# Attention and two gated layers on one core: the tokens' split and turn moved from TensorE to DMA, and two steps on V placed behind a slice

## The chip, the cores and the metric

One core of one Trainium2 chip runs the whole program. The metric is the device time of one execution in microseconds. TensorE (PE) multiplies, VectorE (DVE) and ScalarE (ACT) work on elements, GpSimd (POOL) reduces over partitions, and SyncE (SP) issues every DMA of this kernel on one queue. PEld is TensorE's weight load, which overlaps with its matmuls.

## The reference, cut to what matters

Attention over 4 batches of 8 heads with 576 tokens of width 64, mixed with a retrieval from a memory; then, over all 2304 tokens of width 512, an RMS norm with a gated layer (SiLU), and a second gated layer (sigmoid). The hidden width of both is 1536.

```python
a = softmax(scale * q @ k.T, causal)
attn = g * (phi(q) @ M_prev) / (phi(q) @ z_prev) + (1 - g) * (a @ v)     # per head
x = attn.transpose(0, 2, 1, 3).reshape(2304, 512)
xn = x / sqrt(mean(x * x) + 1e-6) * rms_g
h = silu(xn @ w_gate) * (xn @ w_val)
x = h @ w_out
out = (sigmoid(x @ w_gate2) * (x @ w_val2)) @ w_out2
```

## The kernel before

**Groups.** Tokens are worked in five groups. Group -1 holds the first 128 tokens of all four batches (512 tokens). Groups 0 to 3 hold the other 448 tokens of one batch each. A group runs the two gated layers one after the other (`l` = 0 and 1), and each layer goes over `NF` = 12 slices of 128 hidden units: a gate product (`pg`) and a value product (`pv`), both in `mm3` at L786 with 12 matmuls each, the elementwise part in `hidden` (tanh at L803, products at L805 to L813, a high half on ScalarE at L818 or L822 and a low half on VectorE at L819 or L823), and the slice's share of the output (`po`, `out_share`, L839), which is computed after the products of the next slice. Every operand is split into a high and a low half, so that one product takes three matmuls. Weights pass through a ring of 13 slots (`slot`), three a slice, loaded by SyncE (L753, L756). At the end of a layer `evacuate` empties the four output banks, and in the second layer stores them.

**Attention of the next batch.** While group `g` runs its 24 slices, the attention of group `g + 1` is computed beside it. `att_steps` (L905) yields 36 steps in order: the load of V (`att_v`, L137 and L138), then for the heads `att_qk` (loads and splits q and k) and `att_scores` (scores, maximum over partitions at L501, softmax weights into the single tile `pt`); after head 0's scores `att_vmax` (step 3 counted from 0: five maxima over V at L146, one maximum over partitions, a scale), after head 1's scores `att_vsplit` (step 6: V into a high half on ScalarE, L169, and a low half on VectorE, L170), one head later `att_av` (weighted sum, L517 to L519), and for each pair of heads `att_mem`. The last five steps are `att_norm` (L595 to L588) and four times `next_xT`, which calls `att_xT`. The loop at L1019 emits these steps after the output shares, in proportion to the slices done: in groups 0 to 2 step 3 comes up in slice 3 of the first layer, step 6 in slice 4.

**The tokens' turn.** `att_xT` (L602) takes one tile of 128 tokens: L605 multiplies by the norm and `rms_g` into `xn` (two buffers), four TensorE transposes (L610) turn it into a PSUM tile of the pool `psa` (two buffers, shared with scores and sums), ScalarE copies the fp16 high half out (L614), VectorE subtracts for the low half (L615). The fourth tile of a group gives 64 tokens only. The first gate product of the next group reads all tiles.

**What sets the order.** Each engine runs its instructions in one fixed order. The framework's scheduler lays it out at build time from its own estimate of when each instruction is ready, preferring what was emitted earlier. So an instruction may stand a good deal before or behind the place where it is emitted. `tc.issue_after(i)` keeps all instructions emitted inside it that run on `i`'s engine behind `i` in that engine's order; it adds no semaphore.

Of the kernel before, what the change touches and what calls it, by code (L numbers as in the profile page):

```python
# [9 lines left out]
F32 = mybir.dt.float32  # L10
F32R = mybir.dt.float32r
F16 = mybir.dt.float16
# [4 lines left out]
ALU = mybir.AluOpType  # L17
# [39 lines left out]
def attn_moe_moe_kernel(ctx, tc, qT, kT, qk0, v, mz, beta, w8, rms_g, outT):  # L57
# [6 lines left out]
    nc = tc.nc  # L64
    B, H, D, S = qT.shape
    NP = H // 2
    DM = H * D
    KD = DM // 128
    NF = w8.shape[1]
# [6 lines left out]
    ap_ = ctx.enter_context(tc.tile_pool(name="ap", bufs=1))  # L76
# [7 lines left out]
    ident = const.tile([128, 128], F32, name="ident")  # L84
# [4 lines left out]
        out=tri, in_=tri, compare_op=ALU.is_ge, fill=NEG, base=0, pattern=[[1, 128]], channel_multiplier=-1  # L89
# [35 lines left out]
    for i in range(2):  # L125
        t = const.tile([128, S], F32R, name=f"q2_{i}")
# [6 lines left out]
    st = {}  # L133
# [468 lines left out]
    def att_xT(g, t, xt):  # L602
        s = st[g]
        xn = ap_.tile([128, DM], F32, tag="xn", bufs=2, name="xn")
        nc.vector.scalar_tensor_tensor(  # L605
            out=xn, in0=s["x"][:, t, :], scalar=s["ri"][:, t:t + 1], in1=g_bc, op0=ALU.mult, op1=ALU.mult
        )
        ps = late["ps"].tile([128, KD, 128], F32, tag="pa", name="pxt")
        for k in range(KD):
            nc.tensor.transpose(ps[:, k, :], xn[:, k * 128:(k + 1) * 128], ident)  # L610
        o = 64 if t == 3 else 0
        c0 = 128 * t
        n = 128 - o
        nc.scalar.copy(out=xt[0][:, :, c0:c0 + n], in_=ps[:, :, o:128])  # L614
        nc.vector.tensor_tensor(  # L615
            out=xt[1][:, :, c0:c0 + n], in0=ps[:, :, o:128], in1=xt[0][:, :, c0:c0 + n], op=ALU.subtract
        )


    late, first_raw = {}, []  # L620
    ring = {"w": 0, "top": 0, "raw": 0}
# [45 lines left out]
    def is_half(g, l, f):  # L667
        return g >= 0 and (l == 0 or f >= NWIDE)
# [29 lines left out]
    for i in range(2):  # L698
        t = const.tile([128, 512], I32, name=f"top{i}")
# [82 lines left out]
    def mm3(ps, w, x, n, o=0):  # L782
        i = 0
        for k in range(KD):
            for a, b in ((0, 0), (0, 1), (1, 0)):
                nc.tensor.matmul(  # L786
                    ps[:, 0:n], w[:, a, k * 128:(k + 1) * 128], x[b][:, k, o:o + n], start=(i == 0), stop=(i == 3 * KD - 1)
                )
                i += 1

    def hidden(w, l, f, n, g, x, h, o=0):


        pg = late["mm"].tile([128, NMAX], F32, tag="mm", name="pg")
        mm3(pg, w[0], x, n, o)
        pv = late["mm"].tile([128, NMAX], F32, tag="mm", name="pv")
        mm3(pv, w[1], x, n, o)

        t, hh = h
        t = t[:, o:o + n]  # L800
        half = is_half(g, l, f)
        u = unit[0 if l == 0 else 2][:, f]
        nc.scalar.activation(out=t, in_=pg[:, 0:n], func=AF.Tanh, scale=u[:, 0:1] if half else 0.5)  # L803
        if l == 0:
            nc.vector.scalar_tensor_tensor(out=t, in0=t, scalar=1.0, in1=pg[:, 0:n], op0=ALU.add, op1=ALU.mult)  # L805
            if half:
                nc.vector.scalar_tensor_tensor(  # L807
                    out=t, in0=t, scalar=kappa[:, f:f + 1], in1=pv[:, 0:n], op0=ALU.mult, op1=ALU.mult
                )
            else:  # L810
                nc.vector.tensor_tensor(out=t, in0=t, in1=pv[:, 0:n], op=ALU.mult)
        else:
            nc.vector.scalar_tensor_tensor(out=t, in0=t, scalar=1.0, in1=pv[:, 0:n], op0=ALU.add, op1=ALU.mult)  # L813
        if hh is None:
            return
        hi, lo = hh[:, 0, 0:n], hh[:, 1, 0:n]
        if l == 0 or g < 0:
            nc.scalar.copy(out=hi, in_=t)  # L818
            nc.vector.tensor_tensor(out=lo, in0=t, in1=hi.bitcast(F32), op=ALU.subtract)  # L819
        else:  # L820
            c = u[:, 1:2] if half else 0.5
            nc.scalar.activation(out=hi, in_=t, func=AF.Copy, scale=c)  # L822
            nc.vector.scalar_tensor_tensor(  # L823
                out=lo, in0=t, scalar=c, in1=hi.bitcast(F32), op0=ALU.mult, op1=ALU.subtract
            )
# [70 lines left out]
    def wide_tokens(tags):  # L896

        return [xp.tile([128, KD, NMAX], F32R, tag=t, name="x" + t) for t in tags]

    def half_tokens(tag):  # L900

        t = xp.tile([128, 2, KD, NMAX], F16, tag=tag, name="h" + tag)
        return [t[:, 0], t[:, 1]]

    def att_steps(g):  # L905
        yield lambda: att_v(g)

        for h in range(H + 1):
            if h < H:
                yield lambda h=h: att_qk(g, h)  # L910
                yield lambda h=h: att_scores(g, h)

            if h == 0:
                yield lambda: att_vmax(g)
            if h == 1:
                yield lambda: att_vsplit(g)
            if h > 0:
                yield lambda h=h: att_av(g, h - 1)
                if h % 2 == 0:
                    yield lambda h=h: att_mem(g, h // 2 - 1)  # L920
        yield lambda: att_norm(g, 0, 4)
        for t in range(4):
            yield lambda t=t: next_xT(g, t)
# [33 lines left out]
    def next_xT(g, t):  # L957
        if t == 0:
            st["xt"] = half_tokens("a")
        att_xT(g, t, st["xt"])  # L960

    xt, early_ws, early_hs = att_first()
    zctx.close()
# [11 lines left out]
    for g in range(-1, B):  # L975
        n = 512 if g < 0 else S - 128
        steps = list(att_steps(g + 1)) if g + 1 < B else []

        total = 2 * NF - (6 if g < 0 else 4)

        wait = 1 if g < 0 else 0
        done, used = 0, 0
        for l in range(2):
            early = 2 if g < 0 and l == 0 else 0
            ws, hs = early_ws[:early], early_hs[:early]
            for f in range(early):
                hidden(ws[f], l, f, 256, g, xt, hs[f], 256)
            po = None
            for f in range(NF + 1):
                if f < NF:  # L990
                    if f >= early:
                        if g > 0 and l == 1 and f == NWIDE:
                            mid = NF if g < B - 1 else NF // 2 + 2
                            for e, c in ((nc.vector, slice(NWIDE, mid)), (nc.gpsimd, slice(mid, NF))):
                                if c.start < c.stop:
                                    e.tensor_scalar(
                                        out=unit[2][:, c],
                                        in0=unit[1][:, c],
                                        scalar1=st["half_is1"],
                                        scalar2=None,  # L1000
                                        op0=ALU.mult,
                                    )
                        ws.append(weights(g, l, f))
                        hs.append(htiles(g, l, f))
                        hidden(ws[f], l, f, n, g, xh if l == 1 and is_half(g, l, f) else xt, hs[f])
                if f > 0:
                    if po is None:
                        po = [late[f"po{d // 2}"].tile([128, NMAX], F32, tag=f"po{d}", name="po") for d in range(KD)]
                    out_share(ws[f - 1], hs[f - 1], po, f - 1, n)
                    done += 1  # L1010
                    with ExitStack() as after:

                        if g < 0 and done < 5:
                            traced = nc.cur_bb.bb.instructions
                            for e in (mybir.EngineType.Activation, mybir.EngineType.DVE, mybir.EngineType.SP):
                                after.enter_context(
                                    tc.issue_after(next(i for i in reversed(traced) if i.engine == e))
                                )
                        while used < len(steps) and used < len(steps) * (done - wait) // (total - wait):  # L1019
                            steps[used]()  # L1020
                            used += 1
            if g < 0 and l == 0:
                begin.close()
            xn = wide_tokens("cd") if l == 0 else None
            for d in range(KD):
                evacuate(l, d, n, g, po[d], xn)
            if l == 0 and g >= 0:
                xh = half_tokens("b")
                halve_tokens(n, po, xh)
            if l == 0 and g < 0:  # L1030
                token_scale()
            xt = xn
        xt = st.pop("xt", None)
# [55 lines left out]
```

## Time and profile before

| | us |
|---|---|
| median of 3 runs | 1075.39 |
| lowest to highest | 1075.17 to 1077.75 |
| the profiled execution | 1077.86 |
| its span, first to last instruction | 1076.1 |
| TensorE busy in the span | 1043.3 |
| VectorE busy | 738.0 |
| ScalarE busy | 551.1 |

All rows of the profile below are of that one execution, and their times count from the start of its span. A timeline line gives the start, the length, the engine, the source line, the operation with output and inputs, and the count of merged instructions; the bracket at its end is how long the engine stood before it and what ended that. Lengths of merged matmuls overlap with the next line, because matmuls are pipelined. Waits are put down to the releaser that came last.

### The profile page before, as it was taken

Reading aid. Unit: us, or ns where it says so; the run is one execution under the profiler, and the core shown is the slowest. Engines: PE = TensorE matmul, PEld = TensorE weight load, DVE = VectorE, ACT = ScalarE, POOL = GpSimd, SP = SyncE. Lnnn points to the kernel's source line nnn. Section 1 sums busy time; section 2 is a strip of 40 time slices with the busy share of each in tenths; the row PEclk is TensorE's granted clock in tenths of the full one; section 3 lists DMA queues with packets and bytes.
Section 4 is the critical chain, followed back from the end, with each engine's and each line's share of the span. In section 5 each row is a group of like instructions: output and inputs, shape, how many; then the busy total and the mean of one; then the engine's idle time right before and its main releaser. Section 6 shows DMA issues by size and latency. Waiting matters only on the chain.

```text
span 1076.1 us, 17841 instructions
## 1 busy us (share of the span) xinstructions
PE 1043.3 (97%) x6505; PEld 756.1 (70%) x6509; DVE 738.0 (69%) x1588; ACT 551.1 (51%) x1074; POOL 93.1 (9%) x85
## 2 busy tenths in 40 slices
PE   7899999999899999998999999999999999999998
PEld 5778887888666677665677876766777766667665
DVE  5969999998788788885747876485687653224211
ACT  4768877776587658763434553353346332112111
POOL 2301012000011011100101010000010100000000
PEclk8999999999999999999999999999999999999999
DMA  6499998985567855875547445555554445454440
GB/s 263 149 361 375 323 351 269 329 274 169 191 225 263 284 177 152 283 237 198 166 136 218 149 155 171 183 182 159 186 171 132 132 138 174 146 184 157 142 133 34
DMA packets 90679, 218.49 MB, mean 203 GB/s; under 512 B 10720, under 2 KB 16864, under 8 KB 90464
## 3 DMA queue, kind: packets, MB, share of 16 engines
q1 hardware_dynamic: 90592, 217.36, 61.5%
q8 instruction: 51, 0.84, 0.3%
q14 instruction: 36, 0.29, 0.1%
HBM read 173.28 MB, written 44.04 MB: 202 GB/s over the span
## 4 chain that ended last, share of the span: by engine, by line
PE 71%; DVE 12%; DMA 9%; ACT 4%; issue 3%; SPq 1%; POOL 0%; ACTq 0%; DVEq 0%; POOLq 0%
PE pg L786 21%; PE po L839 21%; PE pv L786 20%; PE ps L206 3%; DMA w<-kept 2%; DMA x<-in_v 1%; DMA rawl<-in_w 1%; DMA g_bc<-in_rms_g 1%; PE pm L566 1%; DMA qd<-in_qT 1%; PE pav L517 1%; PE pav L519 1%; PE pav L518 1%; DVE vl L170 1%; ACT sc L197 1%
## 5 line engine op out<-in xcount | busy, mean ns | idle before, releaser
L803 ACT ACTIVATE t<-pg,unit 128x448 f32<-128x448 f32 x88 | 55.5, 630 | 148.2 <-PE pg L786 148.0
L839 PE MATMUL po<-h,ws 128*128 128x448 f32 (+1 forms) x504 | 121.1, 384 | 0.0
L839 PEld LDWEIGHTS po<-h,ws 128*128 128x128 f32 x504 | 93.3, 188 | 11.9
L501 POOL PARTITION_ALL_REDUCE mb<-mx x32 | 60.2, 1881 | 466.0 <-DVE mx L497 448.7
L786 PEld LDWEIGHTS <-wr 128*128 128x128 f16 x648 | 60.2, 98 | 56.8 <-issue 6.1
L786 PEld LDWEIGHTS <-ws 128*128 128x128 f16 x624 | 58.2, 98 | 54.8 <-issue 5.5
L813 DVE SCALAR_TENSOR_TENSOR t<-t,pv 128x448 f32<-128x448 f32 (+1 forms) x60 | 37.9, 632 | 84.0 <-PE pv L786 83.3
L839 PE MATMUL po<-h,wl 128*128 128x448 f32 (+1 forms) x384 | 93.8, 386 | 0.2 <-DVE h L823 0.2
L839 PE MATMUL po<-h,wr 128*128 128x448 f32 x360 | 83.7, 377 | 0.7 <-DVE h L819 0.7
L786 PEld LDWEIGHTS <-wl 128*128 128x128 f16 x504 | 47.8, 99 | 50.0 <-issue 9.4
L805 DVE SCALAR_TENSOR_TENSOR t<-t,pg 128x448 f32<-128x448 f32 (+2 forms) x60 | 37.2, 620 | 64.4 <-ACT t L803 64.3
L839 PEld LDWEIGHTS po<-h,wl 128*128 128x128 f32 x384 | 71.1, 188 | 9.9 <-DVE h L823 0.6
L473 ACT COPY sc<-ps 128x64 f32<-128x64 f32 (+3 forms) x128 | 47.0, 371 | 57.4 <-DVE sc L468 29.8
L839 PEld LDWEIGHTS po<-h,wr 128*128 128x128 f32 x360 | 67.1, 188 | 8.0 <-DVE h L819 1.1
L818 ACT CAST h<-t 128x448 fp32r<-128x448 f32 (+1 forms) x70 | 40.5, 579 | 55.9 <-DVE t L807 50.5
L206 PE MATMUL ps<-qq,kk 128*128 128x448 f32 (+2 forms) x160 | 57.2, 363 | 7.3 <-ACT sc L473 6.3
L200 DVE TENSOR_TENSOR pt<-sc,pt 128x1536 f16<-128x1536 f32 x32 | 56.1, 1752 | 10.0 <-ACT pt L199 9.8
L197 ACT ACTIVATE sc<-sc 128x1536 f32<-128x1536 f32 x32 | 47.5, 1483 | 22.7 <-DVE sc L510 22.5
L819 DVE TENSOR_TENSOR h<-t,h 128x448 fp32r<-128x448 f32 (+1 forms) x70 | 45.2, 646 | 19.3 <-ACT h L818 18.6
L822 ACT ACTIVATE h<-t,unit 128x448 fp32r<-128x448 f32 x40 | 26.7, 668 | 53.5 <-DVE t L813 53.2
L786 PEld LDWEIGHTS <-wrl 128*128 128x128 f16 x336 | 31.4, 98 | 30.6 <-issue 3.2
L199 ACT CAST pt<-sc 128x1536 f16<-128x1536 f32 x32 | 46.8, 1463 | 4.7 <-PE pav L519 4.6
(245 smaller groups left out, 2484.5 us busy)
## 6 DMA issues: line engine op xcount, KB each, us to landing
raw<-in_w SPq DMA_DIRECT2D x50, 511.8 KB, 6.4
ws<-parts SPq DMA_DIRECT2D x34, 512.0 KB, 3.5
wr<-parts SPq DMA_DIRECT2D x32, 512.0 KB, 3.5
w<-kept SPq DMA_DIRECT2D x50, 256.0 KB, 4.4
kept<-w SPq DMA_DIRECT2D x48, 256.0 KB, 5.4
wl<-parts SPq DMA_DIRECT2D x24, 512.0 KB, 3.5
rawl<-in_w SPq DMA_DIRECT2D x22, 511.8 KB, 6.5
ws<-half SPq DMA_DIRECT2D x41, 256.0 KB, 2.7
```

Source lines behind the costliest of these rows:

```text
L197: nc.scalar.activation(out=sc[:, 0:n], in_=sc[:, 0:n], func=AF.Exp, scale=scale)
L199: nc.scalar.copy(out=pt[:, 0, 0:n], in_=sc[:, 0:n])
L200: nc.vector.tensor_tensor(out=pt[:, 1, 0:n], in0=sc[:, 0:n], in1=pt[:, 0, 0:n], op=ALU.subtract)
L206: nc.tensor.matmul(ps[:, c0:c0 + n], kk[:, k0:k0 + 128], r[:, q0:q0 + n], start=(i == 0), stop=(i == 1 and not mask))
L473: nc.scalar.copy(out=sc[:, d:d + n], in_=ps[:, c:c + n])
L501: nc.gpsimd.partition_all_reduce(mb[:, 0:448], mx[:, 0:448], channels=128, reduce_op=bass_isa.ReduceOp.max)
L786: nc.tensor.matmul(ps[:, 0:n], w[:, a, k * 128:(k + 1) * 128], x[b][:, k, o:o + n], start=(i == 0), stop=(i == 3 * KD - 1))
L803: nc.scalar.activation(out=t, in_=pg[:, 0:n], func=AF.Tanh, scale=u[:, 0:1] if half else 0.5)
L813: nc.vector.scalar_tensor_tensor(out=t, in0=t, scalar=1.0, in1=pv[:, 0:n], op0=ALU.add, op1=ALU.mult)
L818: nc.scalar.copy(out=hi, in_=t)
L819: nc.vector.tensor_tensor(out=lo, in0=t, in1=hi.bitcast(F32), op=ALU.subtract)
L839: nc.tensor.matmul(po[d][:, 0:n], w[2][:, a, c], hh[:, b, 0:n], start=(f == 0 and i == 0), stop=(f == NF - 1 and i == 2))
```

## The change

`att_xT` no longer uses TensorE. ScalarE copies the normed tile `xn` from SBUF into the high half of a new fp16 tile `xs` (one buffer), VectorE subtracts for the low half, and one DMA transpose on SyncE's queue turns both halves, eight blocks of 128 x 128, into the token tile of the next group. `half_tokens` hands out the whole tile as well, so that one DMA can write both halves.

In groups 0 to 2, steps 3 and 6 (`att_vmax`, `att_vsplit`) are emitted inside `issue_after` on the last ScalarE and the last VectorE instruction that `hidden` has just emitted for the slice.

```diff
@@ att_xT
-        ps = late["ps"].tile([128, KD, 128], F32, tag="pa", name="pxt")
-        for k in range(KD):
-            nc.tensor.transpose(ps[:, k, :], xn[:, k * 128:(k + 1) * 128], ident)
+        xs = ap_.tile([128, 2, DM], F16, tag="xs", name="xs")
+        nc.scalar.copy(out=xs[:, 0], in_=xn)
+        nc.vector.tensor_tensor(out=xs[:, 1], in0=xn, in1=xs[:, 0], op=ALU.subtract)
         o = 64 if t == 3 else 0
         c0 = 128 * t
-        n = 128 - o
-        nc.scalar.copy(out=xt[0][:, :, c0:c0 + n], in_=ps[:, :, o:128])
-        nc.vector.tensor_tensor(
-            out=xt[1][:, :, c0:c0 + n], in0=ps[:, :, o:128], in1=xt[0][:, :, c0:c0 + n], op=ALU.subtract
+        nc.sync.dma_start_transpose(
+            out=xt.rearrange("p a k n -> p (a k) n")[:, :, c0:c0 + 128 - o], in_=xs[o:128].rearrange("p a d -> p (a d)")
         )
@@ half_tokens
-        return [t[:, 0], t[:, 1]]
+        return [t[:, 0], t[:, 1], t]
@@ next_xT
-        att_xT(g, t, st["xt"])
+        att_xT(g, t, st["xt"][2])
@@ the loop over groups
         steps = list(att_steps(g + 1)) if g + 1 < B else []
+        values = [steps[k] for k in (3, 6)] if steps else []
...
                         hidden(ws[f], l, f, n, g, xh if l == 1 and is_half(g, l, f) else xt, hs[f])
+                        behind = [
+                            next(i for i in reversed(nc.cur_bb.bb.instructions) if i.engine == e)
+                            for e in (mybir.EngineType.Activation, mybir.EngineType.DVE)
+                        ]
...
                         while used < len(steps) and used < len(steps) * (done - wait) // (total - wait):
-                            steps[used]()
+                            with ExitStack() as late_v:
+                                if g >= 0 and f < NF and steps[used] in values:
+                                    for i in behind:
+                                        late_v.enter_context(tc.issue_after(i))
+                                steps[used]()
                             used += 1
```

## Rows read from the trace of the kernel before

**Rows 1.** The page: TensorE's busy time and share, and the chain by engine.

```profile
PE 1043.3 (97%) x6505; PEld 756.1 (70%) x6509; DVE 738.0 (69%) x1588; ACT 551.1 (51%) x1074; POOL 93.1 (9%) x85
...
PE 71%; DVE 12%; DMA 9%; ACT 4%; issue 3%; SPq 1%; POOL 0%; ACTq 0%; DVEq 0%; POOLq 0%
```

**Rows 2.** Timeline of TensorE where group 0 follows group -1.

```profile
292.66 0.74 PE L206 MATMUL ps<-qq,kk 128*128 128x448 f32 x1 [2.73 <-ACT sc L473]
...
293.58 3.38 PE L786 MATMUL pg<-ha,wl 128*128 128x448 f16 x11
```

**Rows 3.** Timeline of TensorE where group 1 follows group 0.

```profile
487.71 1.04 PE L610 MATMUL pxt<-ident,xn 128*128 128x128 f32 x8
488.50 0.65 PE L839 MATMUL po<-h,wl 128*128 128x448 f32 x2
...
500.36 3.12 PE L839 MATMUL po<-h,wrl 128*128 128x448 f32 x8 [2.14 <-DVE h L823]
...
504.03 2.28 PE L786 MATMUL pg<-ha,wrl 128*128 128x448 f16 x11
...
511.46 0.35 PE L206 MATMUL ps<-qq,kk 128*128 128x192 f32 x1 [2.17 <-ACT sc L473]
```

**Rows 4.** Timeline of TensorE where group 2 follows group 1.

```profile
705.75 2.25 PE L786 MATMUL pg<-ha,wl 128*128 128x448 f16 x11
...
711.51 0.36 PE L206 MATMUL ps<-qq,kk 128*128 128x192 f32 x1 [0.72 <-ACT sc L473]
```

**Rows 5.** Timeline of TensorE where group 3 follows group 2.

```profile
900.52 2.44 PE L786 MATMUL pg<-ha,ws 128*128 128x448 f16 x12
```

**Rows 6.** Timeline of VectorE where group 1 follows group 0.

```profile
482.73 1.42 DVE L605 SCALAR_TENSOR_TENSOR xn<-x,ri,g_bc 128x512 f32<-128x512 f32 x2
...
496.65 3.06 DVE L146 TENSOR_REDUCE am<-x 128x1 f32<-128x512 f32 x5 [2.21 <-DMA x<-in_v]
499.63 0.68 DVE L823 SCALAR_TENSOR_TENSOR h<-t,unit,h 128x448 fp32r<-128x448 f32 x1
...
501.12 0.42 DVE L615 TENSOR_TENSOR ha<-pxt,ha 128x256 f16<-128x256 f32 x1
```

**Rows 7.** What wrote the turned tokens; durations min/median/max in ns, starts, forms.

```profile
L614 ACT CAST ha<-pxt x16: 356/585/592, 282.0 to 893.8; 128x512 f16<-128x512 f32 x12, 128x256 f16<-128x256 f32 x4
L615 DVE TENSOR_TENSOR ha<-pxt,ha x16: 414/680/692, 283.9 to 894.6; 128x512 f16<-128x512 f32 x12, 128x256 f16<-128x256 f32 x4
```

**Rows 8.** Source line L753, loads of 256 KB fp16 weight halves: issue to landing.

```profile
DMA to landing us min/median/max: 2.4/2.7/6.4
```

**Rows 9.** DMA issues: engine, count, KB each, median us to landing.

```profile
half<-wr SPq DMA_DIRECT2D x16, 256.0 KB, 3.1
```

**Rows 10.** Timelines of VectorE where groups 0, 2 and 3 get their first tokens.

```profile
275.59 1.42 DVE L605 SCALAR_TENSOR_TENSOR xn<-x,ri,g_bc 128x512 f32<-128x512 f32 x2
...
685.65 1.41 DVE L605 SCALAR_TENSOR_TENSOR xn<-x,ri,g_bc 128x512 f32<-128x512 f32 x2
...
881.25 1.42 DVE L605 SCALAR_TENSOR_TENSOR xn<-x,ri,g_bc 128x512 f32<-128x512 f32 x2
```

**Rows 11.** Timeline of VectorE around slices 3 and 4 of group 1, first layer.

```profile
533.31 0.62 DVE L819 TENSOR_TENSOR h<-t,h 128x448 fp32r<-128x448 f32 x1 [0.63 <-ACT h L818]
533.85 1.09 DVE L502 TENSOR_TENSOR sc<-sc,mb 128x896 f32<-128x896 f32 x1
534.85 0.95 DVE L510 TENSOR_TENSOR sc<-sc,mb 128x320 f32<-128x320 f32 x3
537.49 0.62 DVE L805 SCALAR_TENSOR_TENSOR t<-t,pg 128x448 f32<-128x448 f32 x1 [1.69 <-ACT t L803]
...
540.41 0.63 DVE L819 TENSOR_TENSOR h<-t,h 128x448 fp32r<-128x448 f32 x1 [0.63 <-ACT h L818]
```

**Rows 12.** Source line L170, the low half of V; columns as in rows 7.

```profile
L170 DVE SCALAR_TENSOR_TENSOR vl<-x,sv,vh x20: 734/742/753, 100.1 to 710.1; 128x512 f16<-128x512 f32 x20
```

**Rows 13.** Source line L517 from 500 to 560 us, head 0's weighted sum in group 1.

```profile
L517 PE MATMUL pav<-vh,pt x14: 192/194/204, 534.3 to 549.4; 128*128 128x65 f16 x14
```

## The prediction

> **What bounds the kernel now.** I read the page's engine shares first, then its chain, and then TensorE's timeline at the four places where a group of 448 tokens begins. TensorE is busy 97% of the span, and the chain runs through it for 71% and through DMA for 9% [rows 1]: only work that TensorE does, or a wait in front of it, is worth anything. Inside the groups its timeline has almost no holes. They sit where one group hands over to the next, and I call these places by the groups on both sides: -1|0, 0|1, 1|2 and 2|3 (group -1 is the one of 512 tokens).
>
> At -1|0 TensorE stands 2.73 us until 292.66 and goes on with the gate product at 293.58, whose eleven matmuls then take 3.38 us [rows 2]; the same eleven take 2.28 at 0|1 [rows 3], so the clock was low behind the hole, for some 1.1 us. At 0|1 there are two holes, 2.14 and 2.17 us, and the gate product goes on at 504.03 [rows 3]. At 1|2 it goes on at 705.75, and a hole of 0.72 follows [rows 4]. At 2|3 there is no hole: 900.52 [rows 5].
>
> Why 2|3 differs is read from VectorE's timeline at 0|1 [rows 6]. The V of the next batch is loaded there, and the five maxima over it stood in VectorE's order ahead of the last slice's low half: VectorE waited 2.21 us for the load, took 3.06 for the maxima, and only at 499.63 made the low half that the last output share waited for; the last two subtractions of the turned tokens came behind that. Group 3 has no next batch. So two things meet at a handover: the chain that turns the tokens (the new group's gate product needs all 448 of them), and V.
>
> **What the change removes.** 64 TensorE transposes. Eight of them hold TensorE from 487.71 to 488.50, 0.79 us [rows 3], so 64 cost 6.3 us, 1.6 in each group's last slices, where TensorE has no holes. They also stood in TensorE's order: at 0|1 the first norm product was there at 483.5 [rows 6] and its transposes came at 487.71 [rows 3]. That wait goes too.
>
> **What it adds.** For each of 16 token tiles a ScalarE copy and a VectorE subtraction from SBUF where they read PSUM before. I price them like those now, 0.585 and 0.68 us [rows 7]; the fourth tile of a group now pays the full width (0.356 and 0.414 before), 16 x 0 plus 4 x 0.5 = 2 us on engines that are not the bound. Then one DMA of 256 KB on SyncE's queue, which turns both halves. No row shows a DMA that turns data. The nearest: 256 KB of fp16 into SBUF lands after 2.4 to 6.4 us, median 2.7 [rows 8]; 256 KB of fp16 out of SBUF lands after 3.1 [rows 9]. I take D = 3.1, since this one reads from SBUF, as the second does, and moves the same bytes; 2.4 and 6.4 are the ends.
>
> On this price the Trainium skill speaks with two voices. "Advanced Engine Details and Errata", section "X-Bar Transpose (TRN2)", says such DMAs are as fast as plain ones; by the 2.7 row the sum below would be 12 us less instead of 6.2. "VectorE: DVE Perf Modes", section "The three transpose paths", gives 1309 ns for one 128x128 block against 390 ns on TensorE, and advises TensorE; eight blocks one behind the other would be an estimated 10.5 us by that page, and the sum an estimated 110 us more than before. No row here shows which; 8 TensorE transposes cost 0.79 us in this trace, far under that page's figure for them.
>
> **The new chain.** There is one split buffer (one name, a pool of one), so tile t+1's copy waits until tile t's DMA has landed. One tile costs 0.585 + 0.68 + D + about 0.15 for the two handoffs (an estimate: gaps of this size are counted as the pipeline's own) = 1.4 + D, four tiles 5.6 + 4D, counted from the end of the first norm product, 0.75 us into the pairs that start at 275.59, 482.73, 685.65 and 881.25 [rows 6, 10]. With D = 3.1 a chain is 18.0 us long.
>
> Each line: chain start + 18.0 = tokens ready; then where the gate product goes on now.
> -1|0: 276.3 + 18.0 = 294.3, against 293.58: 0.8 lost.
> 0|1: 483.5 + 18.0 = 501.5, against 504.03: 2.4 gained (0.1 allowed for the start). The last output share is no longer late, as V is gone from VectorE there, so it is done before 501.5.
> 1|2: 686.4 + 18.0 = 704.4, against 705.75: 1.2 gained.
> 2|3: 882.0 + 18.0 = 900.0, against 900.52: 0.5 gained.
> The transposes' 6.3 us are in these numbers and not added: TensorE reaches the handover 1.6 us sooner and waits there for the tokens.
>
> **V behind its slice.** Steps 3 (maxima, scale) and 6 (split) of the next batch come up in slices 3 and 4 of the first layer. They are now kept behind the last ScalarE and VectorE instructions of that slice's gated product. This removes V from the handovers: the 2.17 us hole at 0|1, ended by a ScalarE copy while both engines split V, and the 0.72 at 1|2. Together 2.9 gained. At -1|0 VectorE did V as well, but the tokens alone would now set the end. In their new place the five maxima (3.06 us) meet a VectorE that ends slice 3's low half at 533.9, has 2.0 us of softmax, and idles 1.69 before slice 4's first product at 537.49 [rows 11]: they fit but for about 1.4 us, which the softmax carries. GpSimd's maximum over partitions moves along; what stands behind it there is the heads' own reduce. The split follows slice 4's low half at 540.41: 5 x 0.742 us [rows 11, 12], done near 545, with ScalarE's five casts beside it. Head 0's weighted sum, which needs it, starts at 534.3 now [rows 13], so it loses up to 10 us and head 1's softmax queues behind it. I take 0 for this: each head's scores have their own place in the order, later than that, and what starts the norm is the last head. The other end is that all 10 us are handed on.
>
> **SyncE.** Each turning DMA waits for its subtraction, and weight loads stand behind it in the same queue; a load takes one slot of 13 and each slice uses three, so it is issued some four slices ahead of its use. I take 0; it costs when the queue is late by more than three slices. A late copy on ScalarE also holds the tanh and the cast behind it; this costs if it is longer than the product and the share that TensorE still has to do, about 4 us.
>
> **Sum.** -0.8 + 2.4 + 1.2 + 0.5 + 2.9 = 6.2 us less. The profiled execution took 1077.86 us with a span of 1076.1; 1077.86 - 6.2 = 1071.7, a ratio of 0.9942. The profile lies 2.5 over the median of the runs, 1075.39, and that times 0.9942 is 1069.2. I forecast **1069**.
>
> **Rivals.**
> Fast turn. If D is 2.4 to 2.7, tokens are ready 1.6 to 2.8 us sooner at each handover; at 2|3 no more than 1.1 can follow. 6.2 + 3 x 1.6 + 1.1 = 12 to 6.2 + 3 x 2.8 + 1.1 = 15.7 less: 1060 to 1063. For: half of the 256 KB loads land within 2.7. The Trainium skill's page "Advanced Engine Details and Errata" would have it so. Against: the writes are short pieces spread over all partitions.
> Serial turn, the slower side. The place is the single split buffer; the price is four times whatever D exceeds, at four handovers: 16 us of time for each us of D. It breaks even at D = 3.5 and decides from there: D = 4.0 gives 14.4 lost against 6.2, 1083.5; D = 4.6 gives 24 - 6.2 and some 3 x 1.1 of low clock behind longer holes, 1096; D = 6.4 gives over 1120. For: D shares queue and rings with the weight loads, and loads took up to 6.4. The Trainium skill's page "VectorE: DVE Perf Modes" would lie beyond even that. Against: both medians in the rows are under 3.5.
> No net change. D near 3.5, or the scheduler, which lays out the order from its own estimates, puts other work into the holes that the change opens: 1073 to 1078. Also the case that the change doesn't do what it says, when V was not what held VectorE.
> V too late. Head 0's 10 us reach the norm in three groups: 30 lost against 6, 1099. For: one buffer of softmax weights makes heads wait for each other. Against: the scores' places.
>
> **Chances.** Forecast (1066 to 1072) 0.35; fast turn 0.17; no net change 0.17; serial turn 0.26; V too late 0.05. What a measurement of this kernel tells from no change is about 0.3%, 3.2 us: faster 0.51, same 0.18, slower 0.31. The range leaves out the fastest turn with its holes all closed and D over 4.6: 1059 to 1096.
>
> **What would show it.** Right: no L610; DMA issues to the turned tokens landing near 3.1 us, four a group, each copy behind the one before; the gate product of the new group going on near 294, 501.5, 704 and 900, less what was gained ahead of it; maxima at slices 3 and 4; no V in the holes. Wrong: a landing over 3.5, SyncE busy for long with one issue, holes over 4 us ahead of the first gate product with a low clock behind them, a norm that comes later in groups 0 to 2, or tanh waiting behind a copy.

## The result, and the profile after

| | before | after |
|---|---|---|
| median of the runs, us | 1076.57 | 1088.94 |
| lowest to highest | 1075.17 to 1078.77 | 1088.61 to 1092.26 |
| the profiled execution | 1077.86 | 1092.26 |
| its span | 1076.1 | 1090.4 |

The changed kernel is slower: 1.012 times the time before, 95% interval 1.0092 to 1.0148. The profiled spans differ by 14.3 us, and the readings below account for that.

The page of the changed kernel: TensorE's busy time, the chain by engine and by line, and from the list of DMA issues the turning DMA (count, median us to landing). Lines from 616 on stand three lower than before; L783 is the gate and value product, L836 the output share.

```profile
PE 1041.4 (95%) x6441; PEld 751.2 (69%) x6445; DVE 744.1 (68%) x1588; ACT 555.6 (51%) x1074; POOL 93.2 (9%) x85
...
PE 79%; DMA 10%; DVE 7%; ACT 2%; issue 2%; SPq 1%; ACTq 0%; POOL 0%; DVEq 0%; POOLq 0%
PE pg L783 23%; PE pv L783 23%; PE po L836 23%; DMA ha<-xs 4%; PE ps L206 4%; DMA w<-kept 2%; PE pm L566 1%; PE pav L517 1%; PE pav L519 1%; DMA kd<-in_kT 1%; PE pav L518 1%; DMA g_bc<-in_rms_g 1%; DVE xs L610 1%; PE po L833 1%; DMA out_T<-o 1%
...
ha<-xs SPq DMA_TRANSPOSE x16, 3.3
```

TensorE's busy time is 1.9 us less [rows 1], where the transposes taken out came to 6.3; matmuls behind the new holes run longer, as shown below, and take part of it back. So TensorE stands 16.2 us more (1090.4 - 1041.4 = 49.0, against 1076.1 - 1043.3 = 32.8), and 16.2 - 1.9 are the 14.3. The turning DMA is on the chain for 4% of the span, some 40 us.

TensorE's timeline at the four handovers, -1|0, 0|1, 1|2 and 2|3; the answer to [rows 2 to 5]:

```profile
294.10 0.63 PE L206 MATMUL ps<-qq,kk 128*128 128x320 f32 x1 [3.31 <-ACT sc L473]
...
305.74 3.78 PE L783 MATMUL pg<-ha,wl 128*128 128x448 f16 x12 [9.27 <-DMA ha<-xs]
...
514.72 0.48 PE L206 MATMUL ps<-qq,kk 128*128 128x448 f32 x1 [2.73 <-ACT sc L473]
...
519.24 4.54 PE L783 MATMUL pg<-ha,wrl 128*128 128x448 f16 x12 [2.53 <-DMA ha<-xs]
...
718.34 0.74 PE L206 MATMUL ps<-qq,kk 128*128 128x448 f32 x1 [2.89 <-DVE sc L468]
...
720.07 4.64 PE L783 MATMUL pg<-ha,wl 128*128 128x448 f16 x12 [0.61 <-issue]
...
914.46 1.08 PE L836 MATMUL po<-h,wrl 128*128 128x448 f32 x4 [0.75 <-ACT h L819]
915.82 2.43 PE L783 MATMUL pg<-ha,ws 128*128 128x448 f16 x12 [0.28 <-DMA ha<-xs]
```

The starts of the gate products cut both executions into stretches, and the difference of the spans falls into them:

| stretch | before | after | difference |
|---|---|---|---|
| start to the gate product at -1\|0 | 293.6 | 305.7 | +12.1 |
| from there to 0\|1 | 210.4 | 213.5 | +3.1 |
| to 1\|2 | 201.7 | 200.8 | -0.9 |
| to 2\|3 | 194.8 | 195.8 | +1.0 |
| to the end | 175.6 | 174.6 | -1.0 |

So one handover, -1|0, lost most of it. TensorE stood 9.27 us there for the turned tokens, and the twelve matmuls behind the hole took 3.78 us where the twelve at 2|3 take 2.43; behind the holes at 0|1 and 1|2 they took 4.54 and 4.64. These three lost 1.4 + 2.1 + 2.2 = 5.7 us, where the kernel before lost 1.1 at -1|0 [rows 2]. The difference of 4.6 is about what the busy time took back (6.3 - 1.9 = 4.4). The granted clock around the hole at -1|0 (columns: stretch, its length, busy time and count of each engine, clock, DMA share, GB/s):

```profile
288.00:306.00 18.00, 3.63 (x11) 2.34 (x12) 12.67 (x32) 11.94 (x27) 4.62 (x4) 0.60 1.11 334
```

A mean of 0.60 is a mix of the two levels, 1.2 and 2.4 GHz; TensorE was busy for 3.63 of these 18 us. Beside it stands a DMA share of 1.11, and that leads to the chain. SyncE's queue, ScalarE's copies and VectorE's subtractions at -1|0:

```profile
277.76 6.08 SPq L613 DMA_TRANSPOSE ha<-xs  x2
284.01 0.46 SPq L137 DMA_DIRECT2D x<-in_v  x1
284.52 0.49 SPq L138 DMA_DIRECT2D x<-in_v  x1
...
290.64 1.03 SPq L685 DMA_DIRECT2D half<-wr  x2
291.99 1.60 SPq L613 DMA_TRANSPOSE ha<-xs  x1
...
298.90 1.32 SPq L182 DMA_DIRECT2D qd<-in_qT  x2
300.32 1.22 SPq L613 DMA_TRANSPOSE ha<-xs  x1
...
281.21 0.60 ACT L609 CAST xs<-xn 128x512 f16<-128x512 f32 x1
...
287.06 0.61 ACT L609 CAST xs<-xn 128x512 f16<-128x512 f32 x1
...
297.74 0.62 ACT L609 CAST xs<-xn 128x512 f16<-128x512 f32 x1 [0.79 <-DMA ha<-xs]
...
289.34 0.69 DVE L610 TENSOR_TENSOR xs<-xn,xs 128x512 f16<-128x512 f32 x1
...
298.39 0.69 DVE L610 TENSOR_TENSOR xs<-xn,xs 128x512 f16<-128x512 f32 x1 [1.49 <-ACT xs L609]
```

The four turning DMAs are issued at 277.76, 282.6 (merged into the first row), 291.99 and 300.32. Behind the second one the load of the next V, 1.25 MB, goes into the same queue (284.01, 284.52), and weight loads and stores follow. The first two DMAs land after 2.9 and 2.7 us. The third lands when the last copy starts, at 297.74, after 5.75; the fourth when the gate product starts, after 5.42. V's load itself landed 6.7 us after its issue, near 291, before the third was issued. And the tiles waited for their turn on three engines. On ScalarE, behind the halving of weights, the second and third copies started 0.5 and 1.8 us after the DMA that they waited for had landed. The third copy ended at 287.67 and its subtraction started at 289.34: 1.67 on VectorE, behind the halving of weights. That ended at 290.03 and the DMA was issued at 291.99: 1.96 on SyncE, behind two stores. The last subtraction ended at 299.08 and its DMA was issued at 300.32: 1.24 behind two q loads.

At 2|3, where no V is loaded, the chain looks like the one forecast. ScalarE's four copies; each waits for the DMA of the tile before it:

```profile
896.80 0.62 ACT L609 CAST xs<-xn 128x512 f16<-128x512 f32 x1 [1.05 <-DVE xn L605]
...
901.97 0.62 ACT L609 CAST xs<-xn 128x512 f16<-128x512 f32 x1 [3.17 <-DMA ha<-xs]
...
906.89 0.62 ACT L609 CAST xs<-xn 128x512 f16<-128x512 f32 x1 [1.14 <-DMA ha<-xs]
...
911.83 0.62 ACT L609 CAST xs<-xn 128x512 f16<-128x512 f32 x1 [2.12 <-DMA ha<-xs]
```

From 896.8 to the gate product at 915.82 is 19.0 us. At 0|1 the copies show V's load once more, here in the wait for the third DMA (issued at 507.23, behind the load at 503.53):

```profile
496.56 0.62 ACT L609 CAST xs<-xn 128x512 f16<-128x512 f32 x1 [1.35 <-DVE xn L605]
...
513.50 0.62 ACT L609 CAST xs<-xn 128x512 f16<-128x512 f32 x1 [3.09 <-DMA ha<-xs]
```

513.50 - 507.23 = 6.27 us, and 22.7 us from the first copy to the gate product. At 1|2 the third DMA, behind V's load too, lands after 6.3 us, and the chain is 21.1 us long (698.94 to 720.07). Finally V itself: its five maxima start at 333.2, 546.4 and 748.7, at slice 3 as the change wants, where they started at 290.1, 496.7 and 699.2.

### The profile page after: what moved, and what is told of

It reads as the page before. It is cut to its first block, busy times and chain, and to the rows that moved or that the text cites. A ratio compares the mean times of both kernels' runs of the same rounds, so it can differ in the third digit from the quotient of the medians.

```text
span 1090.4 us, 17741 instructions
## 1 busy us (share of the span) xinstructions
PE 1041.4 (95%) x6441; PEld 751.2 (69%) x6445; DVE 744.1 (68%) x1588; ACT 555.6 (51%) x1074; POOL 93.2 (9%) x85
## 4 chain that ended last, share of the span: by engine, by line
PE 79%; DMA 10%; DVE 7%; ACT 2%; issue 2%; SPq 1%; ACTq 0%; POOL 0%; DVEq 0%; POOLq 0%
PE pg L783 23%; PE pv L783 23%; PE po L836 23%; DMA ha<-xs 4%; PE ps L206 4%; DMA w<-kept 2%; PE pm L566 1%; PE pav L517 1%; PE pav L519 1%; DMA kd<-in_kT 1%; PE pav L518 1%; DMA g_bc<-in_rms_g 1%; DVE xs L610 1%; PE po L833 1%; DMA out_T<-o 1%
## 5 line engine op out<-in xcount | busy, mean ns | idle before, releaser
L836 PE MATMUL po<-h,ws 128*128 128x448 f32 (+1 forms) x504 | 120.6, 384 | 0.0
L836 PEld LDWEIGHTS po<-h,ws 128*128 128x128 f32 x504 | 93.8, 188 | 12.4
L783 PEld LDWEIGHTS <-wr 128*128 128x128 f16 x648 | 60.5, 99 | 59.9 <-issue 9.4
L836 PE MATMUL po<-h,wl 128*128 128x448 f32 (+1 forms) x384 | 94.7, 388 | 2.8 <-DVE hb L856 2.8
L783 PEld LDWEIGHTS <-ws 128*128 128x128 f16 x624 | 58.0, 98 | 56.2 <-issue 7.6
L783 PEld LDWEIGHTS <-wl 128*128 128x128 f16 x504 | 48.4, 100 | 60.3 <-issue 19.1
L836 PE MATMUL po<-h,wr 128*128 128x448 f32 x360 | 84.1, 378 | 0.0
L836 PEld LDWEIGHTS po<-h,wl 128*128 128x128 f32 x384 | 71.9, 190 | 12.5 <-DVE hb L856 3.1
L836 PEld LDWEIGHTS po<-h,wr 128*128 128x128 f32 x360 | 67.1, 188 | 6.9
L473 ACT COPY sc<-ps 128x448 f32<-128x448 f32 (+3 forms) x128 | 46.9, 372 | 46.5 <-DVE sc L468 26.0
L206 PE MATMUL ps<-qq,kk 128*128 128x448 f32 (+2 forms) x160 | 56.9, 362 | 14.3 <-ACT sc L473 10.0
L200 DVE TENSOR_TENSOR pt<-sc,pt 128x1536 f16<-128x1536 f32 x32 | 56.2, 1755 | 12.4 <-ACT pt L199 12.3
L783 PEld LDWEIGHTS <-wrl 128*128 128x128 f16 x336 | 32.1, 99 | 34.2 <-issue 7.4
```

What stands on the lines that cost most here:

```text
L200: nc.vector.tensor_tensor(out=pt[:, 1, 0:n], in0=sc[:, 0:n], in1=pt[:, 0, 0:n], op=ALU.subtract)
L206: nc.tensor.matmul(ps[:, c0:c0 + n], kk[:, k0:k0 + 128], r[:, q0:q0 + n], start=(i == 0), stop=(i == 1 and not mask))
L473: nc.scalar.copy(out=sc[:, d:d + n], in_=ps[:, c:c + n])
L783: nc.tensor.matmul(ps[:, 0:n], w[:, a, k * 128:(k + 1) * 128], x[b][:, k, o:o + n], start=(i == 0), stop=(i == 3 * KD - 1))
L836: nc.tensor.matmul(po[d][:, 0:n], w[2][:, a, c], hh[:, b, 0:n], start=(f == 0 and i == 0), stop=(f == NF - 1 and i == 2))
```

## The experiments

Theories: "turn" or "serial", the single split buffer makes the four tiles a chain that ends behind TensorE's need; "crowded queue", the load of V and other loads on SyncE's queue lengthen it; "V", the moved steps delay the attention. Each run is given as the median, the median of the kernel before on the same chip, and the ratio with its interval.

**The turn alone** (`e1`), V where the scheduler puts it:

```diff
-                                if g >= 0 and f < NF and steps[used] in values:
+                                if False:
```

> The turn by DMA alone; the two steps on V stay where the scheduler puts them. Theory 'turn' (the single split buffer and its queue cost the time): as slow as the changed kernel or slower, 1088 to 1096, since V is back in the handovers. Theory 'V' (moving V behind its slice delays the attention and costs the time): 1070 to 1076.

Measured: 1086.4 against 1079.3, ratio 1.0069 (1.0054 to 1.0085): under the range of theory "turn" and far over that of theory "V". The turn alone is slower than the kernel before, so V's move is not the main cause. The hole at -1|0 is there too:

```profile
306.10 3.97 PE L783 MATMUL pg<-ha,wl 128*128 128x448 f16 x12 [6.83 <-DMA ha<-xs]
...
517.98 3.84 PE L783 MATMUL pg<-ha,wrl 128*128 128x448 f16 x12 [2.04 <-DMA ha<-xs]
...
713.59 2.45 PE L783 MATMUL pg<-ha,wl 128*128 128x448 f16 x12
```

But with V's move on top the ratio is 1.012 (1.0092 to 1.0148), and the intervals don't meet: on the serial turn V's move costs about 0.5%. In the two profiles it shows from 0|1 to 1|2, 195.6 us here and 200.8 in the changed kernel, and the first norm product comes 173.5 and 178.9 us behind the gate product. Why was not tested.

**V's move alone** (`e2`), TensorE transposes as before (the edit is shown against the changed kernel):

```diff
-        xs = ap_.tile([128, 2, DM], F16, tag="xs", name="xs")
...
-        nc.sync.dma_start_transpose(
...
+        ps = late["ps"].tile([128, KD, 128], F32, tag="pa", name="pxt")
+        for k in range(KD):
+            nc.tensor.transpose(ps[:, k, :], xn[:, k * 128:(k + 1) * 128], ident)
...
```

> The two steps on V behind their slice alone; the tokens are turned on TensorE as before. Theory 'turn': faster than before, since the handovers at 0|1 and 1|2 lose their holes of 2.14, 2.17, 0.98 and 0.72 us: 1069 to 1073. Theory 'V': slower than before, 1082 or more.

Measured: 1068.7 against 1079.3, ratio 0.9902 (0.9885 to 0.9919): 10.6 us faster, a little beyond the expectation. The gate products go on without the holes of [rows 2 to 4]:

```profile
290.41 2.24 PE L786 MATMUL pg<-ha,wl 128*128 128x448 f16 x11
...
501.60 2.25 PE L786 MATMUL pg<-ha,wrl 128*128 128x448 f16 x11
...
695.81 2.44 PE L786 MATMUL pg<-ha,wl 128*128 128x448 f16 x12
```

The stretches from these rows: 290.4 to the first (before: 293.6), 211.2 (210.4), 194.2 (201.7). The last one also holds 17 matmuls fewer, and the next is longer, 197.4 (194.8). By the pages TensorE stands 3.7 us less than before (1068.6 - 1039.5 = 29.1 for 32.8) and is busy 3.8 us less with as many matmuls. So the two parts pull against each other: V's move gains 1%, and the turn, put on top of it, loses 2%.

**Three split buffers** (`e3`). They share the ring of a weight tile that only the first two slices of group -1 use:

```diff
-        xs = ap_.tile([128, 2, DM], F16, tag="xs", name="xs")
+        xs = late["h"].tile([128, 2, DM], F16, tag="wo", bufs=3, name="xs")
...
-                raw = late["h"].tile([128, 512], F32, tag="wo", bufs=2, name="wo")
+                raw = late["h"].tile([128, 512], F32, tag="wo", bufs=3, name="wo")
```

> The changed kernel with three split buffers in place of one, so that a tile's copy doesn't wait for the DMA of the tile before it. Theory 'serial' (the buffer makes the chain): the chains of 19 to 29 us shrink by two or three DMA times each, the gate product starts 6 to 12 us sooner at -1|0 and 3 to 6 at 0|1 and 1|2: 1070 to 1077. Theory 'crowded queue' (the load of V and the weight loads make each turning DMA late): 1084 or more.

Measured: 1065.7 against 1079.3, ratio 0.9868 (0.9845 to 0.9892), faster than the kernel before and the changed one, and beyond the range expected of theory "serial". TensorE at -1|0, 0|1 and 1|2, the four copies at -1|0, and the landing of its turning DMAs (min/median/max):

```profile
288.99 2.43 PE L783 MATMUL pg<-ha,wl 128*128 128x448 f16 x12 [2.64 <-DMA ha<-xs]
...
502.64 2.43 PE L783 MATMUL pg<-ha,wrl 128*128 128x448 f16 x12 [1.06 <-DMA ha<-xs]
...
695.61 2.24 PE L783 MATMUL pg<-ha,wl 128*128 128x448 f16 x11 [0.88 <-ACT sc L473]
...
275.32 0.62 ACT L609 CAST xs<-xn 128x512 f16<-128x512 f32 x1 [3.00 <-DVE xn L605]
...
277.20 0.61 ACT L609 CAST xs<-xn 128x512 f16<-128x512 f32 x1
...
279.56 0.61 ACT L609 CAST xs<-xn 128x512 f16<-128x512 f32 x1
...
280.69 0.61 ACT L609 CAST xs<-xn 128x512 f16<-128x512 f32 x1
...
DMA to landing us min/median/max: 3.0/4.1/8.0
```

The starts of the four copies lie within 5.4 us (275.32 to 280.69) where they took 21.4 in the changed kernel (276.38 to 297.74), and the gate product starts at 288.99 in place of 305.74. A single DMA lands later than in the changed kernel (median 4.1 against 3.3), while several are under way at once. What counted was that they waited for each other, not what one takes.

**The load of V behind the last turning DMA** (`e4`), one buffer:

```diff
+            if "turn" in st:
+                behind_turn.enter_context(tc.issue_after(st["turn"]))
             nc.sync.dma_start(out=x[:, 0:4, :], in_=v[g, 0:512, :].rearrange("(t s) d -> s t d", s=128))
...
+        st["turn"] = next(i for i in reversed(nc.cur_bb.bb.instructions) if i.engine == mybir.EngineType.SP)
```

> The changed kernel with the load of the next V queued behind the last turning DMA of the group on SyncE. Theory 'crowded queue': the turning DMAs that took 5 to 6 us behind that load land in about 3, which gives 3 to 5 us at each of three handovers: 1075 to 1081. Theory 'serial': at most 1 us a handover, 1086 to 1089.

Measured: 1079.6 against 1079.3, ratio 1.0 (0.9988 to 1.0012). That is 1.2% under the ratio of the changed kernel, as the theory of the crowded queue expects. Its turning DMAs and its gate products at -1|0 and 0|1:

```profile
DMA to landing us min/median/max: 2.5/2.9/4.8
...
301.40 4.09 PE L787 MATMUL pg<-ha,wl 128*128 128x448 f16 x12 [7.51 <-DMA ha<-xs]
...
512.92 2.36 PE L787 MATMUL pg<-ha,wrl 128*128 128x448 f16 x6 [0.75 <-DMA ha<-xs]
```

The longest landing fell from 6.3 to 4.8 us. From the first copy to the gate product it is 26.1, 19.9, 17.8 and 18.8 us at the four handovers (29.4, 22.7, 21.1 and 19.0 in the changed kernel): about 3 less wherever a V is loaded. At -1|0 the last two DMAs land after 4.0 and 4.4 us, in place of 5.7 and 5.4. The hole at -1|0 is still 7.51 us, so V's load is not all of it.

**Both** (`e5`): the edits of `e3` and `e4` together.

> Three split buffers, and the load of the next V behind the last turning DMA. If the load of V costs only because it stands inside a serial chain, this is no faster than three buffers alone, 1064 to 1068. If it delays the tokens in any case, 2 to 4 us faster, 1061 to 1064.

Measured: 1067.9 against 1077.3, ratio 0.9899 (0.9875 to 0.9923). Not faster than three buffers alone: outside the serial chain V's load shows no cost in the time. In its profile the gate product at -1|0 starts sooner, at 285.75, and the stretch behind it is longer, 217.1.

**Two split buffers** (`e6`): as `e3` with `bufs=2`.

> The changed kernel with two split buffers. Theory 'serial': with two, tile t waits for the DMA of tile t-2, so a chain holds two DMA times in place of four; most of the gain is there: 1066 to 1072. If any wait for a turning DMA costs, half of it: 1075 to 1080.

Measured: 1070.1 against 1077.3, ratio 0.9932 (0.9908 to 0.9956). Most of the gain is there, and three are better by 0.6%. At -1|0 the gate product starts where it does with three:

```profile
289.03 3.31 PE L783 MATMUL pg<-ha,wl 128*128 128x448 f16 x9 [2.18 <-DMA ha<-xs]
```

**A plain DMA in place of the turning one** (`e7`), one buffer; the turn itself is left out:

```diff
-        nc.sync.dma_start_transpose(
-            out=xt.rearrange("p a k n -> p (a k) n")[:, :, c0:c0 + 128 - o], in_=xs[o:128].rearrange("p a d -> p (a d)")
+        nc.sync.dma_start(
+            out=xt.rearrange("p a k n -> p (a k) n")[:, :, c0:c0 + 128 - o],
+            in_=xs.rearrange("p a (k n) -> p (a k) n", n=128)[:, :, o:128],
         )
```

> The changed kernel, one split buffer, with a plain DMA of the same bytes in the same 256-byte pieces in place of the turning one; the turn itself is left out. If the turning costs by itself: issue 0.3 to 0.6 us in place of 1.25 on SyncE, landing under 2.7, 8 us or more faster than the changed kernel. If the DMA's time is that of its bytes, pieces and queue: landing near 3.3 and 1085 to 1091.

Measured: 1088.9 against 1077.3, ratio 1.0101 (1.0083 to 1.0119), the changed kernel's ratio. The DMA of the plain run and of the changed kernel: duration of its issue on SyncE (ns) and us to landing, min/median/max.

```profile
L613 SPq DMA_DIRECT2D ha<-xs x16: 606/652/697, 275.3 to 911.2; - x16
...
DMA to landing us min/median/max: 2.6/3.3/7.4
...
L613 SPq DMA_TRANSPOSE ha<-xs x16: 1196/1250/1597, 277.8 to 913.2; - x16
...
DMA to landing us min/median/max: 2.4/3.3/6.3
```

The issue is cheaper, 0.65 against 1.25 us; the median landing is the same. That the data are turned is not what costs.

**Three buffers, V early** (`e8`): the edits of `e3` and `e1` together.

> Three split buffers, with the two steps on V where the scheduler puts them. With one buffer the move of V was worth nothing (1086.4 without it, 1088.9 with it); with TensorE transposes it was worth 10 us. If it is worth something only where the tokens are not the later of the two, this is slower than three buffers with V moved, 1071 to 1076. If its worth with TensorE transposes came from elsewhere, 1064 to 1068.

Measured: 1069.6 against 1077.3, ratio 0.9913 (0.989 to 0.9937), 1.4 us under the time expected of one reading and 1.6 over that of the other, so between the two. Beside three buffers with V moved (0.9868, and 0.987 in a second timing below) the move is worth about 0.45% here; the intervals touch.

**V late in groups 1 and 2 alone** (`e9` with three buffers, `e10` with TensorE transposes): `if g >= 1 and ...` in place of `if g >= 0 and ...`.

> Three split buffers, and the two steps on V behind their slice in groups 1 and 2 alone. In group 0, where VectorE still halves the weights, the stretch between first gate products was 213.6 us with V late and 209.8 with V early; in group 1 it was 193.0 with V late and 197.6 early. If these two differences are V's, this is 3 to 4 us faster than three buffers with V late in all groups: ratio 0.983 to 0.985. If they are the scheduler's reordering at large, within 2 us of it: 0.985 to 0.990.

> TensorE transposes as before, V behind its slice in groups 1 and 2 alone. Beside the run above it tells what the turn by DMA is worth once its buffers don't bind: by TensorE's time alone 6 us, so ratio 0.989 to 0.993 here; if the turn's waits at the handovers eat that, within 2 us of the run above. It keeps V in the handover at -1|0, which had a hole of 2.73 us.

Measured: `e9` 1068.2 against 1079.2, ratio 0.9893 (0.9872 to 0.9915); `e10` 1068.4, ratio 0.9894 (0.9878 to 0.991). `e9` is not faster than `e3`, so the expectation that V's place in group 0 costs 4 us falls. It was built on one profile: in that of `e11` below, the kernel of `e3` once more, the stretch of 213.6 us is 210.6. The two runs are equal.

**The best two again** (`e11` is the kernel of `e3`, `e12` that of `e2`), side by side:

> Three split buffers with V moved in all three groups, timed beside the TensorE turn with V moved. If the turn by DMA is worth its 6.3 us of TensorE time once the buffers don't bind: ratio 0.984 to 0.987. If its chain and queue waits eat that gain: 0.988 to 0.991, the same as the other run.

> The TensorE turn with V moved in all three groups, the partner of the run above: ratio 0.989 to 0.991 by its first timing. The difference of the two is what the turn by DMA is worth without the single buffer.

Measured: 1065.3 and 1067.7 against 1079.9, ratios 0.987 (0.9845 to 0.9895) and 0.9892 (0.9869 to 0.9916). The turn by DMA is 2.4 us ahead here and 3.0 in the first timing. The intervals of the ratios overlap; but the two ran side by side on one chip, and all five times of `e11` (1063.2 to 1066.7) lie under all six of `e12` (1066.9 to 1068.6). So with three buffers and V moved in all groups the turn by DMA is worth some 2 to 3 us, less than its 6.3 us of transposes, and in the pair `e9` and `e10` nothing. In the two profiled executions, 4.2 us apart, TensorE is busy 6.6 us less in `e11` (1032.5 against 1039.1) and stands 2.4 more (28.9 against 26.5). Its waits for the last turning DMA at -1|0 and 0|1, 2.60 + 0.99 us, would account for that; no run tested it.

```profile
288.18 2.43 PE L783 MATMUL pg<-ha,wl 128*128 128x448 f16 x12 [2.60 <-DMA ha<-xs]
...
498.81 2.43 PE L783 MATMUL pg<-ha,wrl 128*128 128x448 f16 x12 [0.99 <-DMA ha<-xs]
```

## Why the prediction was wrong

**What bounds, and where the time goes: right.** Of the 14.3 us, 12.1 lie ahead of the gate product at -1|0, where TensorE stands for the tokens.

**The duration D: right as a median, wrong where it counted.** 3.1 was forecast and 3.3 measured. But at 0|1 and 1|2 the DMA behind V's load took 6.3, and at -1|0 two among weight loads and stores took 5.7 and 5.4. Both ends of the range, 2.4 and 6.4 [rows 8], were nearly met, and the mean of the sixteen is 3.8. The forecast took one D for all sixteen. It had V's load in front of it: the maxima waited 2.21 us for it at 0|1 [rows 6], and the change moves the maxima, not the load. With the load behind the turn the ratio falls from 1.012 to 1.0 (`e4`).

**"1.4 + D" for a tile: the step that failed most.** It has no term for the three queues that a tile passes. At 2|3 this did no harm, 18.0 forecast and 19.0 measured. At -1|0 the tiles stood 1.67 + 1.96 + 1.24 = 4.9 us in the orders of VectorE and SyncE and 2.3 in ScalarE's, among the halving of weights and the stores and loads that go with it: 7.2 us, priced at nothing. The four DMAs landed after 2.9 + 2.7 + 5.7 + 5.4 = 16.7 us in place of 12.4. Together they make the chain 29.4 us long, 11.4 over the forecast. The prediction spoke of weight loads behind a waiting turn on SyncE, and not of turns behind other DMAs.

So -1|0 came out 12.1 us later where 0.8 was laid out, and the stretches that end at the other three handovers came out 3.1 later, 0.9 sooner and 1.0 later where 2.4, 1.2 and 0.5 sooner stood, besides the 2.9 for V. The four chains are 11.4, 4.7, 3.1 and 1.0 us over 18.0, 20.2 in all; with them the prediction's own sum gives 20.2 - 6.2 = 14.0 us more, where the profiled spans differ by 14.3. That it comes so near is in part luck: the low clock behind the longer holes, about 4.6 us, is not in that sum.

**V's move: right in kind, wrong in place.** 2.9 us was forecast and added to the rest. Alone it gains 10.6 (`e2`), more than three times that; 3.7 less of TensorE's standing show in its profile, near the forecast, and as much again of busy time, which the forecast did not price. On top of the serial turn it gains nothing and costs 0.5% (1.012 with it, 1.0069 without). The prediction added two gains at the same handovers. That the later of two waits decides there, the tokens', explains a gain of nothing; it does not explain a loss, and with three buffers (`e8`) the move was worth 0.45%, less than that reading expected. So this part is argued and not shown.

**The rivals.** The serial turn it was, with a chance of 0.26; its place was right, as `e3` shows: with three buffers the same change gains 1.3%. Its price was not: it was laid out as 16 us for each us of D, evenly over four handovers, which by the mean D of 3.8 would be 10.9 lost against 6.2; more came, and most of it at one handover. V too late falls as the main cause by `e1` and `e2`; a part of about 5 us, on the serial turn alone, is left by `e1`. The Trainium skill's pages: that a turning DMA is as fast as a plain one ("Advanced Engine Details and Errata", section "X-Bar Transpose (TRN2)") agrees with `e7`, 3.3 and 3.3 us. The Trainium skill's 1309 ns for a block ("VectorE: DVE Perf Modes", section "The three transpose paths") does not add up block by block here: eight blocks land in 3.3 us.

**Weight loads on SyncE, work behind a late copy: taken at 0.** At 0|1, 1|2 and 2|3 no hole of TensorE's between the first copy and the gate product waits for a weight load or for the tanh. But three stand behind a late copy in another way. At 0|1 ScalarE stood 3.09 us for the third DMA, and a score copy came behind the tokens' copy in its order; at 1|2 VectorE stood 2.91 for the last copy, with score work behind it:

```profile
514.46 0.64 ACT L473 COPY sc<-ps 128x64 f32<-128x64 f32 x2
...
716.67 0.69 DVE L610 TENSOR_TENSOR xs<-xn,xs 128x512 f16<-128x512 f32 x1 [2.91 <-ACT xs L609]
```

TensorE's holes of 2.73 and 2.89 us shown above end with that work, and the 0.75 at 2|3 comes about in the same way. The last tokens landed later still at each (519.2, 719.9 and 915.7), so the gate product itself was not later for them. Not tested alone.

**What stays open.** The 3.1 us that group 0 lost in the changed kernel can't be told from none: in the same stretch the kernel of `e3` took 213.6 us in one profile and 210.6 in another (`e11`, 498.81 - 288.18), and that of `e2` 211.2 and 209.3 (`e12`). Open is why V's move costs 0.5% on the serial turn, and why it gains more alone than its holes. Each edit makes the scheduler lay out another order, and differences of 2 us between two profiles can't be put down to the edit.

## What to carry to other kernels

Before work moves from an engine to a DMA, count the buffers between them: with one, every tile pays the DMA's whole time from issue to landing and each queue on its way, and a large load that falls into that chain costs again (1.2% here). Price such a chain at the most crowded place where it runs, not by the median of a DMA. Don't add gains at the same handover without testing each alone: here V's move was worth 10 us with one partner and cost 5 with the other.

## What the runs showed of the hardware

A DMA that turns 256 KB of fp16 within on-chip memory lands as soon as a plain one of the same bytes in 256-byte pieces (median 3.3 us both, over sixteen of which four move half as much) and holds SyncE twice as long (1.25 against 0.65 us; a 256 KB weight load 0.32). Behind a hole of 9.27 us, in a stretch with a granted clock of 0.60, twelve matmuls took 3.78 us where they take 2.43 at a granted clock of 1.00; behind the holes at 0|1 and 1|2 they took 4.54 and 4.64, at 0.53 and 0.50.
